# Second half of tile 0's second layer as seven quarter-size products, with its sums and those of w_out made earlier on VectorE

## The chip, the cores and the metric

The kernel runs on one core of one Trainium2 chip. A core has five engines that each run their own list of instructions in order and meet through semaphores: TensorE (PE, with its weight loads shown apart as PEld), VectorE (DVE), ScalarE (ACT), GpSimd (POOL) and SyncE (SP, which here only issues DMAs). TensorE works from SBUF into PSUM, eight banks of 2 KB for each of the 128 partitions; VectorE and ScalarE read PSUM, GpSimd does not in this kernel. The metric is the device time of one execution in microseconds; less is better.

## The reference: banded attention, then a two-layer MLP with a Gelu

Everything the kernel must compute is in these lines (q, k, v: 8 batches, 8 heads, 576 positions, 64 per head; x has 4608 tokens of 512 features; the hidden layer has 2048):

```python
scores = scale * np.matmul(q, k.transpose(0, 1, 3, 2))
mask = np.abs(pos[:, None] - pos[None, :]) <= 32
attn = softmax(np.where(mask, scores, -1e9))          # over the last axis
x = (attn @ v).transpose(0, 2, 1, 3).reshape(4608, 512)
h = x @ w_in                                          # 512 -> 2048
g = h * (1.0 / (1.0 + np.exp(-1.702 * h)))
out = g @ w_out                                       # 2048 -> 512
```

## The kernel before

**Tiles and units.** The 4608 tokens are 36 units of 128 (shifted by 32 positions, so that a unit's band of keys spans two blocks), and 9 tiles of 512, four units each. For a unit, `scores` makes q k^T on TensorE into PSUM, ScalarE takes the exponential (line 263), `band` multiplies the mask in on VectorE (line 271), `values` multiplies with v on TensorE, `norm` divides on VectorE (lines 300 and 301), and `x_T` or `x_T2` turns the result into x transposed, with a copy from PSUM.

**Layer 1** (`w_in`, Gelu). Tile 0 does it plainly (`layer1_plain`, in eight pieces d of two feature blocks each and two halves of 256 tokens). From tile 1 on, a group of features n (0 to 3) is made by `l1_group` with seven products P1 to P7 of half size in each dimension in place of eight, in the manner of Strassen and Winograd. Its operands are sums: `w1_sums` of w_in (tiles a1 to a4, in two halves), `x_sums` of x. A group uses four PSUM banks A, C, B, E. Its order on TensorE is P1 (into A), fill, P7 (into C), fill, P6 (into B), P2 (into A), fill, P5 (into B), P4 (into E), fill, P3 (into B). ScalarE copies A into B and C into an SBUF tile s7 after P7. VectorE makes e = b + s7 after P6 (line 439, called the E add) and c = b + s7 after P5 (line 445, the C add). So P5 may not write B before line 439 has read it, P3 not before line 445, and P4 needs the sum in E. ScalarE takes the four Gelus (line 426).

**Fill and side.** `fill(i)` puts matmuls of the second layer, from the list `self.l2`, behind product i; `dv` is a list of VectorE instructions, of which `fill` and `side` take the next ones at fixed places. A place in the group is also a place in VectorE's own order: what a fill adds after P1 and P7 stands ahead of the E add, what side 0 and the fill after P2 add stands between the E add and the C add.

**Layer 2** (`w_out`). For tile 0 it is plain: `layer2_plain(0, pr)` for each half pr of the token blocks, 32 matmuls of 512 columns for a half, two PSUM banks LA and LB, each copied out after its sixteenth feature block. From tile 1 on, `layer2` makes a `pair` (tile, half) by seven products of eight matmuls each, with 256 columns; it needs sums of w_out (`w2_sums`, tiles b1 to b4, two halves of 1,024 elements each) and of g (`g_sums`, which makes three sums in a tile gs and overwrites one quarter of g). A pair uses the same LA and LB, in halves: P1 and P2 add up in a, P7 in c, the others in b and e; after P7 ScalarE or VectorE (`seed2`) copies a into b and c into s7o, after P6 VectorE adds (line 519), after P2 a copy goes out (line 521), after P5 an add goes out (line 525), after P3 the 512-wide rest goes out (line 534).

**The order of the work around the change** is written out by hand (`manual_schedule`: every engine runs its instructions as the program emits them). `opening` does tile 0 up to its first layer and 24 of the 32 matmuls of its second layer's first half, with the attention of tile 1. `first_layer1` then runs the four groups of tile 1; its fills take the last eight matmuls of the first half in group 0 and 24 of the 32 of the second half in the groups 1 to 3. In VectorE's list, group 0 has the two last sums of w_in, later groups have `g_sums` of tile 1 and the eight `w2_sums`. `run` then emits the scores of units 8 and 9, the last eight matmuls of the second half, the scores of unit 10, the first twelve of the list `more` (the pairs from tile 1 on, whose first item is P1 of tile 1), the masks of units 8 and 9, and so on. GpSimd issues the loads of q, k and v (`fetch`) and makes the copies of v for odd blocks (`odd_v`, lines 216 and 217); the second layer's results leave through SP (`store`).

Of the kernel before, what the change touches and what calls it, by code (L numbers as in the profile page):

```python
# [26 lines left out]
class _Kernel:  # L27
# [333 lines left out]
        return [lambda: sub(s[:, 2], b22, b12), lambda: sub(s[:, 0], b12, b11), lambda: sub(s[:, 1], b22, s[:, 0]),  # L361
                lambda: sub(s[:, 3], b21, s[:, 1])]

    def g_sums(self, t, lo, n):

        e = self.nc.vector
        g = self.g[t]
        if t not in self.gs:
            self.gs[t] = self.sb("gs", [128, 3, 8, 256], F16, 2)
        s = self.gs[t]  # L370
        f, f2 = slice(lo, lo + n), slice(8 + lo, 8 + lo + n)
        a11, a21, a12, a22 = g[:, f, 0:256], g[:, f, 256:512], g[:, f2, 0:256], g[:, f2, 256:512]
        return [lambda: e.tensor_add(s[:, 0, f], a21, a22),
                lambda: e.tensor_sub(a21, a11, a21),
                lambda: e.tensor_sub(s[:, 1, f], s[:, 0, f], a11),
                lambda: e.tensor_sub(s[:, 2, f], a12, s[:, 1, f])]
# [122 lines left out]
    def layer2(self, pairs, last):  # L499

        dve = self.nc.vector

        def pair(t, pr, la="LA", lb="LB", end=None):
            st = {}

            def after(P):  # L510
                o = st.get("o")
                if P == 7:
                    be = self.bank(lb, name="o")
                    st.update(b=be[:, 0:256], e=be[:, 256:512], be=be, s7=self.sb("s7o", [128, 256], F32, 2),
                              o=self.sb("o_sb", [128, 2, self.DM], F32, 2))
                    self.copy(self.seed2, st["b"], st["a"])
                    self.copy(self.seed2, st["s7"], st["c"])
                elif P == 6:
                    dve.tensor_add(st["e"], st["b"], st["s7"])
                elif P == 2:  # L520
                    self.copy(self.l2eng, o[:, 0, 0:256], st["a"])
                    if end:
                        self.store_part(t, pr, o, 0, slice(0, 256), end[0])
                elif P == 5:
                    dve.tensor_add(o[:, 1, 256:512], st["b"], st["s7"])
                    if end:
                        self.store_part(t, pr, o, 1, slice(0, 512), end[0])
                elif P == 4 and end:
                    self.copy(self.nc.scalar, o[:, 1, 0:256], st["e"])
                elif P == 3 and end:  # L530
                    self.copy(end[1], o[:, 0, 256:512], st["b"])
                    self.store_part(t, pr, o, 0, slice(256, 512), end[0])
                elif P == 3:
                    self.copy(self.l2eng, o.rearrange("p i n -> p (i n)")[:, 256:768], st["be"])
                    self.store(t, pr, o)

            def part(P, f):
                if P == 1 and f == 0:
                    ac = self.bank(la, name="o")
                    st.update(a=ac[:, 0:256], c=ac[:, 256:512])  # L540
                bank = st["a" if P in (1, 2) else "c" if P == 7 else "e" if P == 4 else "b"]
                self.l2_mm(t, pr, P, f, bank, start=(P == 1))
                if f == 7:
                    after(P)

            return {P: [lambda P=P, f=f: part(P, f) for f in range(8)] for P in (1, 7, 6, 2, 4, 5, 3)}

        ps = [pair(*x) for x in pairs[:-1]] + [pair(*pairs[-1], end=(self.nc.sync, dve))]
        out = ps[0][1] + ps[0][7]
        for x, y in zip(ps, ps[1:]):  # L550
            out += x[6] + x[2] + x[4] + x[5] + y[1] + x[3] + y[7]
        x, y = ps[-1], pair(*last, "A", "B", (self.nc.scalar, self.nc.scalar))
        out += y[1] + y[7]
        for P in (6, 2, 4, 5, 3):
            out += x[P] + y[P]
        return out
# [12 lines left out]
    def opening(self):  # L569

        nc, dve, act, pool = self.nc, self.nc.vector, self.nc.scalar, self.nc.gpsimd
# [56 lines left out]
        h, n, gelus = [], [0], []  # L628

        def l1(half, *ds):  # L630
            for d in ds:
                self.layer1_plain(0, d, half, h[n[0] % len(h)])
                n[0] += 1
# [66 lines left out]
        h[:] = "BE"  # L700
        n[0] = 0
        l1(1, 6, 7)
        self.x_T2(4, "A", act)
        self.do(self.l2, 4)
        self.x_T2(6, "t", dve)
# [11 lines left out]
    @staticmethod  # L717
    def do(fs, n=99):
        for _ in range(min(n, len(fs))):
            fs.pop(0)()  # L720
# [76 lines left out]

    def run(self):
        pool, act = self.nc.gpsimd, self.nc.scalar
        self.l2 = self.layer2_plain(0, 0) + self.layer2_plain(0, 1)  # L800
        self.opening()
        self.do(self.x_sums(1))
        late = self.first_layer1()
        more = self.layer2([(i, j) for i in range(1, self.NT) for j in range(2)][:-1], (self.NT - 1, 1))
        do = self.do
        self.l2eng = dve = self.nc.vector
        self.seed2 = act
        self.scores(8, "t")
        self.scores(9, "AC")
        self.turn(14)  # L810
        self.turn(15)
        do(late, 2)
        do(self.l2)
        self.l2 = more
        self.scores(10, "BE")
        do(more, 12)
        self.band(8)
        self.band(9)
        do(late)
        do(more, 4)  # L820
        self.values(8, "t")
        self.values(9, "AC")
        self.odd_v(12, pool)
        self.odd_v(13, pool)
        self.fetch(16)
        self.fetch(17)
        self.norm(8)
        self.norm(9)
        do(more, 8)
        self.band(10)  # L830
        self.scores(11, "BE")
        do(more, 8)
        self.x_T2(8, "t", act)
        self.values(10, "AC")
        self.norm(10)
        do(more, 8)
        self.scores(12, "t")
        self.scores(13, "BE")
        self.band(11)
        self.values(11, "AC")  # L840
        self.norm(11)
        do(more, 4)
        self.scores(14, "t")
        self.x_T2(10, "C", dve)
        self.scores(15, "BE")
        do(self.x_sums(2))
        self.seed2 = dve
        late = self.back(2)
        for t in range(3, self.NT):
            self.front(t, late)  # L850
            late = self.back(t)
        self.l2eng = act
        self.do(late, 2)
        self.do(self.l2, 16)
        self.do(late)
        self.do(self.l2, 999)

    def first_layer1(self):

        dv = [lambda i=i: self.w1_sums((i,), 1) for i in (2, 4)]  # L860
        for n in range(4):
            if n == 3:
                self.turn(12)
                self.turn(13)
            self.odd_v(8 + n, self.nc.gpsimd)
            self.fetch(12 + n)

            def fill(i):
                self.do(self.l2, {1: 1, 7: 1, 2: 3, 4: 3}[i])
                self.do(dv, {1: 2, 7: 1, 2: 0, 4: 2}[i] if n else 0)  # L870
                if i == 7 and n:
                    self.T_pe([("k8", "q8", "k9"), ("q9", "k10", "q10"), ("k11", "q11", "k12")][n - 1], self.nc.scalar)

            self.l1_group(1, n, fill, lambda i: self.do(dv, 1))
            dv += self.g_sums(1, 2 * n, 2)
            if n in (0, 1):
                dv += [lambda i=i, j=j: self.w2_sums((i,), j) for i in ((3, 1), (2, 4))[n] for j in range(2)]
        return dv

@with_exitstack  # L880
# [44 lines left out]
```

## Time and profile before

| | before |
|---|---|
| median of 3 runs | 286.68 us (286.27 to 287.21) |
| the profiled execution, its own time | 286.05 us |
| its span in the trace | 284.3 us |
| what lies around the span | 1.75 us |
| TensorE clock granted | 1.00 |
| tile 1's four groups | 46.91 to 68.50 us of the span |

A row of the timeline reads: start in us, busy time in us, engine, source line, operation, output tile from input tiles, partitions x elements and type, and how many instructions the row merges; in brackets is the idle time of the engine just before and what ended it. Line 70 is the helper that issues every matmul, so there one goes by the tiles: h is the first layer, o the second, sc scores, pv values, tp a transpose. Line 67 is the helper for copies. Matmuls are pipelined, so busy times of neighbours overlap and the distance from start to start is the cost of one.

### The profile page before, as it was taken

What the parts mean: (1) busy time and instruction counts of PE and PEld (TensorE: products, weight loads), DVE (VectorE), ACT (ScalarE), POOL (GpSimd) and SP (SyncE); (2) the same over time, 40 slices, a digit from 0 to 9 for tenths busy, and PEclk for the clock granted to TensorE, in tenths of its full rate; (3) what the DMA queues carried; (4) which work ended last, traced back from release to release, by engine and by line L of the source; (5) the groups of instructions that cost most, each with busy time, mean ns of one, the idle gap of its engine ahead of it and who ended that gap; (6) DMA issues with size and microseconds to landing.
All of it is one profiled execution on the core that took longest, in us unless ns stands there. A gap on an engine that the chain in (4) does not pass through costs nothing.

```text
span 284.3 us, 9219 instructions
## 1 busy us (share of the span) xinstructions
PE 275.4 (97%) x3818; PEld 229.8 (81%) x3818; DVE 217.0 (76%) x500; ACT 193.7 (68%) x340; POOL 128.8 (45%) x195
## 2 busy tenths in 40 slices
PE   7799999999999999999999999999999999999994
PEld 7678847776777888888888888888888888888883
DVE  1758896897887978797879887888788878945631
ACT  2467785789787769667966896588758775567410
POOL 8966467897699719749075909330110000000000
PEclk9999999999999999999999999999999999999999
DMA  7999999999999999999999999994422031201033
GB/s 93 186 193 198 186 202 158 195 124 133 133 171 154 182 130 189 150 201 147 194 106 169 141 201 106 194 112 114 130 59 94 3 111 21 76 0 74 2 112 115
DMA packets 147003, 37.38 MB, mean 131 GB/s; under 512 B 133904, under 2 KB 142608, under 8 KB 146960
## 3 DMA queue, kind: packets, MB, share of 16 engines
q0 software_dynamic: 104480, 18.42, 95.0%
q1 hardware_dynamic: 42032, 17.84, 32.6%
q8 instruction: 30, 0.49, 0.7%
q10 hardware_dynamic: 448, 0.52, 0.6%
q14 instruction: 13, 0.11, 0.1%
HBM read 36.83 MB, written 9.44 MB: 163 GB/s over the span
## 4 chain that ended last, share of the span: by engine, by line
PE 87%; DVE 4%; ACT 3%; DMA 2%; issue 1%; POOL 1%; DVEq 0%; ACTq 0%; POOLq 0%
PE h L70 39%; PE o L70 37%; PE pv L70 4%; PE sc L70 3%; DMA ve<-in_v_dram 2%; DVE p L271 2%; DVE x L301 1%; ACT p L263 1%; PE tp L329 1%; ACT L263 1%; PE junk L70 1%; PE tp L189 1%; PE tp L239 1%; POOL ve L199 1%; ACT g L426 1%
## 5 line engine op out<-in xcount | busy, mean ns | idle before, releaser
L426 ACT ACTIVATE g<-h 128x512 f16<-128x512 f32 x128 | 72.2, 598 | 35.8 <-PE h L70 35.0
L70 PEld LDWEIGHTS <-g 128*128 128x128 f16 x576 | 54.3, 98 | 9.9 <-DMA w<-in_moe_w_out_dram 0.4
L70 PEld LDWEIGHTS <-a 128*128 128x128 f16 x512 | 49.3, 97 | 10.9 <-issue 0.8
L70 PE MATMUL h<-xs,a 128*128 128x256 f16 x384 | 57.6, 272 | 0.1
L70 PE MATMUL o<-w,g 128*128 128x256 f16 (+1 forms) x320 | 55.3, 294 | 0.1
L70 PEld LDWEIGHTS <-w 128*128 128x128 f16 x512 | 48.9, 98 | 6.8 <-DVE xT L67 0.2
L70 PE MATMUL h<-xT,w 128*128 128x256 f16 x384 | 54.0, 273 | 0.0
L199 POOL DMA_DIRECT2D ve<-in_v_dram x39 | 33.3, 857 | 37.8 <-issue 30.8
L70 PEld LDWEIGHTS <-gs 128*128 128x128 f16 x384 | 36.8, 98 | 5.3 <-issue 0.4
L263 ACT ACTIVATE p<-sc 128x512 bf16<-128x512 f32 x72 | 36.7, 617 | 3.2 <-PE sc L70 3.1
L70 PE MATMUL o<-b,gs 128*128 128x256 f16 x256 | 37.7, 273 | 0.5 <-ACT o L67 0.5
L70 PE MATMUL o<-b,g 128*128 128x256 f16 x256 | 37.3, 273 | 0.0
L439 DVE TENSOR_TENSOR h<-h,s 128x512 f32<-128x512 f32 x32 | 22.3, 698 | 18.5 <-PE h L70 18.5
L67 ACT COPY h<-h 128x512 f32<-128x512 f32 x32 | 18.8, 588 | 15.9 <-PE h L70 15.5
L131 POOL DMA_DIRECT2D qst<-in_q_dram x35 | 28.1, 805 | 2.3 <-DMA w<-in_moe_w_out_dram 1.7
L131 POOL DMA_DIRECT2D kst<-in_k_dram x31 | 26.5, 856 | 5.7 <-DMA ve<-in_v_dram 3.9
L301 DVE TENSOR_TENSOR x<-pv,rec 128x256 f16<-128x256 f32 (+1 forms) x53 | 27.6, 520 | 1.8
L271 DVE TENSOR_TENSOR p<-p,mask 128x1024 bf16<-128x1024 bf16 x36 | 24.6, 687 | 4.1 <-ACT p L263 4.1
L445 DVE TENSOR_TENSOR h<-h,s 128x512 f32<-128x512 f32 x32 | 22.4, 700 | 4.7 <-PE h L70 4.2
L216 POOL COPY vo<-ve 64x264 int32<-64x264 int32 x29 | 14.0, 482 | 25.8 <-PE pv L70 24.7
L67 ACT COPY s<-h 128x512 f32<-128x512 f32 x32 | 19.2, 599 | 1.3
L70 PE MATMUL h<-xs,w 128*128 128x256 f16 x128 | 19.2, 273 | 0.0
(86 smaller groups left out, 367.6 us busy)
## 6 DMA issues: line engine op xcount, KB each, us to landing
out_dram<-o_sb SPq DMA_DIRECT2D x33, 256.0 KB, 4.0
ve<-in_v_dram POOLq DMA_DIRECT2D x31, 128.0 KB, 6.5
kst<-in_k_dram POOLq DMA_DIRECT2D x25, 128.0 KB, 6.5
qst<-in_q_dram POOLq DMA_DIRECT2D x21, 128.0 KB, 5.9
w<-in_moe_w_in_dram POOLq DMA_DIRECT2D x4, 512.0 KB, 8.2
w<-in_moe_w_out_dram POOLq DMA_DIRECT2D x4, 512.0 KB, 12.3
qst<-in_q_dram POOLq DMA_DIRECT2D x7, 96.0 KB, 6.7
ve<-in_v_dram POOLq DMA_DIRECT2D x10, 64.0 KB, 7.9
```

The lines of the kernel that those rows point to most:

```text
L67: (eng.copy if eng is self.nc.scalar else eng.tensor_copy)(out, in_)
L70: self.nc.tensor.matmul(out, lhsT, rhs, start=start, stop=stop, skip_group_check=True)
L131: self.nc.gpsimd.dma_start(t[off:off + n], src[b, :, s:s + n, :].rearrange("h s d -> s h d"))
L189: self.nc.tensor.transpose(tp[64 * (h % 2):64 * (h % 2) + 64, h // 2, j, :], src[:, 4 * i + h, j, :], self.ident)
L199: self.nc.gpsimd.dma_start(t[off:off + n, :, :self.D], self.v[b, :, s:s + n, :].rearrange("h s d -> s h d"))
L216: eng.tensor_copy(words(vo[64:128]), words(self.ve[u % 9][64:128]))
L263: self.nc.scalar.activation(p[:, eo].rearrange("k h s -> k (h s)"), sc[eo], AF.Exp, scale=self.scale)
L271: (eng or self.nc.vector).tensor_mul(pv, pv, msk.to_broadcast([128, 8, 2, SQ]))
L301: dve.tensor_mul(x[:, 4 * at:4 * (at + n), :].rearrange("p (b h) d -> p b h d", b=n), acc[:, :, :, :D], r.to_broadcast([128, n, 4, D]))
L426: act.activation(g[:, f, 256 * half:256 * half + 256], bank.rearrange("p (i n) -> p i n", i=2), AF.Gelu_apprx_sigmoid)
L439: dve.tensor_add(e, b, s7)
L445: dve.tensor_add(c, b, s7)
```

## The change

Tile 0's second half (token blocks pr = 1) is made like the later tiles: `self.l2` holds `layer2_plain(0, 0)` alone, and `layer2` now also builds a pair (0, 1) whose 56 matmuls of 256 columns (`self.lead`, in the order P1, P7, P6, P2, P4, P5, P3) come after it. `g_sums` gets a column offset and width, and makes the sums of tile 0 for the half's 128 columns in two calls of four feature blocks, each with four VectorE instructions of 512 elements: one call in `opening`, after the last pieces of tile 0's first layer, one at the head of `dv`. The list `dv` starts with these four, then `w2_sums` of b3, the two sums of w_in, and the other six `w2_sums`, then `g_sums` of tile 1 as they come. Group 0 takes five of them in place of two; the later groups take one more each, in the fill after P2. A fill of the groups 1 to 3 takes twice as many matmuls, of half the columns. In the groups, VectorE's list runs: group 0, four quarter sums and a first b3; group 1, the second b3, two sums of w_in ahead of the E add, two of b1 ahead of the C add, then three of b2 and b4; group 2, the last of b4 and then `g_sums` of tile 1.

```diff
-    def g_sums(self, t, lo, n):
+    def g_sums(self, t, lo, n, p=0, w=256):
...
-        s = self.gs[t]
+        s = self.gs[t][:, :, :, p:p + w]
...
-        a11, a21, a12, a22 = g[:, f, 0:256], g[:, f, 256:512], g[:, f2, 0:256], g[:, f2, 256:512]
+        a11, a21, a12, a22 = g[:, f, p:p + w], g[:, f, 256 + p:256 + p + w], g[:, f2, p:p + w], g[:, f2, 256 + p:256 + p + w]
...
+        x = pair(0, 1)
+        self.lead = x[1] + x[7] + x[6] + x[2] + x[4] + x[5] + x[3]
...
         l1(1, 6, 7)
+        self.do(self.g_sums(0, 0, 4, 128, 128))
         self.x_T2(4, "A", act)
...
-        self.l2 = self.layer2_plain(0, 0) + self.layer2_plain(0, 1)
+        self.l2 = self.layer2_plain(0, 0)
+        more = self.layer2([(i, j) for i in range(1, self.NT) for j in range(2)][:-1], (self.NT - 1, 1))
+        self.seed2 = self.l2eng = act
         self.opening()
...
-        dv = [lambda i=i: self.w1_sums((i,), 1) for i in (2, 4)]
+        self.l2 += self.lead
+        dv = self.g_sums(0, 4, 4, 128, 128)
+        dv += [lambda j=j: self.w2_sums((3,), j) for j in range(2)]
+        dv += [lambda i=i: self.w1_sums((i,), 1) for i in (2, 4)]
+        dv += [lambda i=i, j=j: self.w2_sums((i,), j) for i in (1, 2, 4) for j in range(2)]
...
-                self.do(self.l2, {1: 1, 7: 1, 2: 3, 4: 3}[i])
-                self.do(dv, {1: 2, 7: 1, 2: 0, 4: 2}[i] if n else 0)
+                self.do(self.l2, {1: 2, 7: 2, 2: 6, 4: 6}[i] // (1 if n else 2))
+                self.do(dv, {1: 2, 7: 1, 2: 1, 4: 2}[i] if n else {1: 0, 7: 0, 2: 1, 4: 2}[i])
...
-            if n in (0, 1):
-                dv += [lambda i=i, j=j: self.w2_sums((i,), j) for i in ((3, 1), (2, 4))[n] for j in range(2)]
```

More of the change, by code (lines that the diff above doesn't have):

```diff
@@ L803, in run @@
         late = self.first_layer1()
-        more = self.layer2([(i, j) for i in range(1, self.NT) for j in range(2)][:-1], (self.NT - 1, 1))
         do = self.do
         self.l2eng = dve = self.nc.vector
-        self.seed2 = act
         self.scores(8, "t")
```

## The prediction

> **What bounds the kernel now.** I read the page first, then busy time by stretch, then PE, DVE and ACT in order of time from 43 to 78 us, where the change lies. The page gives TensorE nearly the whole span:
>
> ```profile
> PE 275.4 (97%) x3818; PEld 229.8 (81%) x3818; DVE 217.0 (76%) x500; ACT 193.7 (68%) x340; POOL 128.8 (45%) x195
> ```
>
> The next view has a row for each stretch; these two are the groups 1 and 2 of the four feature groups of tile 1's first layer, group 0 to group 3. The columns are length, then busy time and count of PE, PEld, DVE, ACT, POOL, then clock. PE fills each stretch at clock 1.00, but DVE is busy 4.60 of 5.63 us in group 1 and 5.20 of 5.60 in group 2: about 1.0 and 0.4 us are free.
>
> ```profile
> 51.74:57.37 5.63, 5.61 (x50) 4.19 (x48) 4.60 (x10) 4.90 (x10) 4.89 (x8) 1.00 1.99 206
> 57.37:62.97 5.60, 5.60 (x50) 4.19 (x48) 5.20 (x10) 4.82 (x10) 5.44 (x9) 1.00 1.40 118
> ```
>
> DVE runs its list in the written order, and two of its instructions in each group gate PE: line 439 (the "E add", reads bank B after product P6) must end before P5 writes B, and line 445 (the "C add", after P5) before P3. PE in groups 1 and 2 (start, length, operation):
>
> ```profile
> 52.36 0.38 PE L70 MATMUL o<-w,g 128*128 128x512 f16 x1
> 52.57 0.60 PE L70 MATMUL h<-xs,a 128*128 128x256 f16 x4
> 53.89 0.60 PE L70 MATMUL h<-xs,a 128*128 128x256 f16 x4
> 55.41 0.60 PE L70 MATMUL h<-xs,a 128*128 128x256 f16 x4
> 56.93 0.60 PE L70 MATMUL h<-xT,a 128*128 128x256 f16 x4
> 57.37 0.60 PE L70 MATMUL h<-xT,w 128*128 128x256 f16 x4
> 59.35 0.60 PE L70 MATMUL h<-xs,a 128*128 128x256 f16 x4
> 60.22 0.81 PE L70 MATMUL o<-w,g 128*128 128x512 f16 x3
> 61.02 0.60 PE L70 MATMUL h<-xs,a 128*128 128x256 f16 x4
> 62.54 0.60 PE L70 MATMUL h<-xT,a 128*128 128x256 f16 x4
> ```
>
> In group 1, P7 starts at 52.57, P6 at 53.89, P5 at 55.41 and P3 at 56.93: P6 to P5 and P5 to P3 are 1.52 us each when nothing waits. In group 2 they are 59.35, 61.02 and 62.54: P6 to P5 took 1.67. The DVE rows, with idle time before an instruction in brackets:
>
> ```profile
> 50.42 0.70 DVE L445 TENSOR_TENSOR h<-h,s 128x512 f32<-128x512 f32 x1 [0.16 <-PE h L70]
> 51.02 0.68 DVE L343 TENSOR_TENSOR a<-w,a 128x1024 f16<-128x1024 f16 x1
> 51.62 1.28 DVE L67 COPY o_sb<-o 128x512 f32<-128x512 f32 x2
> 54.60 0.70 DVE L439 TENSOR_TENSOR h<-h,s 128x512 f32<-128x512 f32 x1 [0.57 <-PE h L70]
> 56.05 0.70 DVE L445 TENSOR_TENSOR h<-h,s 128x512 f32<-128x512 f32 x1 [0.43 <-PE h L70]
> 56.66 2.90 DVE L353 TENSOR_TENSOR b<-w 128x1024 f16<-128x1024 f16 x4
> 59.49 0.41 DVE L373 TENSOR_TENSOR gs<-g 128x512 f16<-128x512 f16 x1
> 60.27 0.69 DVE L439 TENSOR_TENSOR h<-h,s 128x512 f32<-128x512 f32 x1
> ```
>
> The E add of group 2 at 60.27 had no idle time before it: DVE came late to it from four sums of w_out, and P5 could start only at 61.02, 0.74 after the add. The three matmuls before P5 start at 60.22 and need 0.64 (1.52 less two products of 0.44, the distance 56.93 to 57.37), so PE lost about 0.15 us. This sets the rules I use: E add no sooner than P6 + 0.71 (53.89 to 54.60), C add no sooner than P5 + 0.64 (55.41 to 56.05), and each lets P5 or P3 go 0.74 after its start. The same 0.74 separates the first copy at 51.62 from PE's 52.36, which needed the bank that it frees.
>
> **The change part by part.** *The products.* Removed are 32 matmuls of 512 columns, added 56 of 256. In the groups 1 to 3 each fill keeps its length (two of 256 for one of 512); all of the gain lies in the last piece, where eight of 256 take the place of these eight of 512:
>
> ```profile
> 67.99 0.60 PE L70 MATMUL h<-xT,a 128*128 128x256 f16 x4
> 69.15 1.90 PE L70 MATMUL o<-w,g 128*128 128x512 f16 x8
> 70.98 0.45 PE L70 MATMUL sc<-qT,kT 64*64 64x64 bf16 x24
> 71.40 1.03 PE L70 MATMUL o<-w,g 128*128 128x256 f16 x8
> 72.27 1.04 PE L70 MATMUL o<-b,g 128*128 128x256 f16 x8
> ```
>
> 69.15 to 70.98 less a small gap is 1.7 us; eight of 256 take 0.87 (71.40 to 72.27): 0.83 us of PE work goes.
>
> *Four quarter sums in the opening.* DVE waits there 2.21 us for PE:
>
> ```profile
> 46.25 0.69 DVE L67 COPY xT<-tp 128x1024 f16<-128x1024 f16 x1 [2.21 <-PE tp L329]
> ```
>
> A sum of 512 elements takes 0.39 from start to start (59.49 to 60.27 above is two, one after the other), taken as 0.40, four 1.6: hidden, cost 0. They write into the buffer that tile 0's staged q and k left, whose last readers are the scores of unit 3, long done. Uncovered they cost at most 0.4: at 0.66 each, as one such sum took at 69.26 (row below), they end at 46.67.
>
> *Group 0.* Its two sums of w_in go later. In the order of the new code, after the C add at 50.42 DVE has one quarter sum (51.02 to 51.42) in place of 0.60 of w_in. So the two copies that free banks LA and LB start at 51.42, not 51.62. LA is free at 52.16 and PE, ready at 52.18 (group 1's P1 ran its 0.44 from 51.74), no longer waits: 0.18 gained.
>
> *Group 1.* DVE's list between the C add of group 0 and the E add of group 1 is now: quarter sum, two copies, quarter sum, then w_out, w_out, w_in, w_in with 1,024 elements each. At 0.60 each (51.02 to 51.62): 51.42 + 1.20 + 0.40 + 4 x 0.60 = 55.42. P6 is due at 53.71 and its E add at 54.42, so the add is 1.0 late, and P5 goes at 55.42 + 0.74 = 56.16 in place of 55.41. PE stands still 0.9 us; queued behind P5 on PE are P4, the fill and P3, behind the add on DVE two sums of w_out and the C add. Those two sums start at 56.02. I take them at 0.71, the mean of the four at 56.66 (to 59.49), because they fall beside the same two copies on POOL, which begin at 56.69 (below, with shortest, median and longest ns of the two lines):
>
> ```profile
> 56.69 0.92 POOL L216 COPY vo<-ve 64x264 int32<-64x264 int32 x1
> L216 POOL COPY vo<-ve x29: 407/408/920, 19.6 to 210.0; 64x264 int32<-64x264 int32 x29
> L217 POOL COPY vo<-ve x28: 402/403/760, 20.1 to 199.7; 64x264 int32<-64x264 int32 x28
> ```
>
> The C add starts at 57.44, P3 at 58.18 against 56.93. Running total: 1.25 us late. At 0.60 per sum it would be 1.03.
>
> The Trainium skill (SBUF — State Buffer, Who interferes with whom) says that a VectorE instruction with two SBUF inputs and a GpSimd one that reads SBUF lock each other out for a whole instruction. By it the two POOL copies could come before the C add as a whole, which is rival 3 below, and the sum would be +1.7 in place of +1.1. The four sums at 56.66 lost 0.43 in all (2.83 against 2.40), which bears out the contention, not the full price here.
>
> *Group 2.* P1 at 58.62, P6 1.98 later (57.37 to 59.35) at 60.60, E add due at 61.31. DVE after the C add: four sums of w_out (2.4) and two of tile 1 (0.8), to 61.24: in time, so the 0.15 wait of before is gone and P5 starts at 62.12. From 61.91 DVE has a sum, the new 256-wide add (0.34, as 75.98 to 76.31 below), a sum: C add at 63.05, P3 at 63.79, against 62.54: still 1.25.
>
> *Group 3* holds five sums, the two adds and a new 256-wide add, some 3.6 us in 5.5: no stall, P3 at 69.2 against 67.99.
>
> *ACT* gets three 256-wide copies (0.45 each by the row at 73.90 below) and loses one of 512. The two seeds in group 1 stand ahead of the Gelu of bank C, but that one waits for the late C add; next P7 needs C at 59.28, it is free at 59.2. Taken at 0; without that cover, up to 0.3. *Queues*: no DMA is added; the half tile's store leaves SP after a copy at the end of P3, as it did after the last of the eight, and only a later use of its buffer waits for it: 0.
>
> *The end of the stage*, in the times of before:
>
> ```profile
> 70.54 2.07 ACT L263 ACTIVATE p<-sc 128x512 bf16<-128x512 f32 x4
> 72.46 0.62 ACT L67 COPY o_sb<-o 128x512 f32<-128x512 f32 x1
> 73.90 0.45 ACT L67 COPY o<-o 128x256 f32<-128x256 f32 x1
> 74.40 1.03 PE L70 MATMUL o<-b,gs 128*128 128x256 f16 x8 [0.46 <-ACT o L67]
> 69.26 0.66 DVE L373 TENSOR_TENSOR gs<-g 128x512 f16<-128x512 f16 x1 [0.67 <-ACT g L426]
> 72.64 0.69 DVE L271 TENSOR_TENSOR p<-p,mask 128x1024 bf16<-128x1024 bf16 x1 [0.22 <-ACT p L263]
> 75.98 0.42 DVE L519 TENSOR_TENSOR o<-o,s7o 128x256 f32<-128x256 f32 x1
> 76.31 0.68 DVE L271 TENSOR_TENSOR p<-p,mask 128x1024 bf16<-128x1024 bf16 x1
> 77.17 0.22 PE L70 MATMUL pv<-ve,p 128*64 128x65 bf16 x1
> ```
>
> PE already waits here (0.46) for ACT, whose four exps, behind a table load, PE's shorter list doesn't touch: they follow the last Gelu, which follows P3. The copy at 72.46 leaves ACT, so the seed and the P6 behind it come 0.45 sooner. But the mask at 72.64 still waits for the exps, and DVE's list from it to the mask at 76.31 is unchanged; unit 10's values, at 77.17 before, need that mask: 76.31 + 0.73 = 77.04. Of 0.83, 0.13 stays (0.45 if DVE's list runs shorter). From 80 us on PE's longest wait for another engine is this row, so nothing absorbs the shift:
>
> ```profile
> PE tp L329 <- DVE x L301: 0.2, 1, 0.2
> ```
>
> **Sum.** +1.25 (the late adds, gains of 0.18 and 0.15 inside) - 0.13 = +1.1 us. On the profiled execution, 286.05 us, that is 287.15; that execution lies 0.63 under the median of the runs, 286.68, so for the median 287.8. Its own bounds: low 1.0 - 0.45 = +0.55 (287.2); high 1.25 + 0.4 = +1.65 (288.3).
>
> **The rivals.**
> 1. *The adds stay in time*: DVE passes its longer list quickly enough that neither add reaches PE. It takes 0.9 us less than my 4.4 us ahead of the E add of group 1; for it speaks only that 0.57 and 0.43 were idle there. Then -0.18 - 0.15 - 0.13 = about -0.5: 286.2.
> 2. *Faster*: the values of unit 10 are not what holds the end of the stage, PE keeps the whole 0.83 and DVE is in time as in 1: -0.83 - 0.33 = -1.16, 285.5. It decides if the mask at 76.31 can start 0.7 sooner; the unbroken DVE list from 72.64 speaks against it.
> 3. *Slower still*: DVE stands still ahead of the C add of group 1 for both POOL copies at their shortest, 0.41 + 0.40, of which 0.71 per sum holds 0.22: +0.6, with up to 0.4 on top where the opening's sums aren't hidden: +1.7 to +2.1, 288.4 to 288.8. For it speaks POOL's slow copy of 0.92; against it, that the four sums beside it lost only 0.43. By the rule of the Trainium skill (SBUF — State Buffer, Who interferes with whom) it would come out so.
>
> **How the numbers follow.** Forecast 0.60 (its range 287.2 to 288.3), rival 1 0.15, rival 2 0.08, rival 3 0.17. A difference of 0.3% is 0.86 us, about what this kernel's measurement can tell; +0.86 is 287.54, so of the forecast's 0.60 some 0.43 is slower and 0.17 the same. Slower 0.60, same 0.32, faster 0.08. The range leaves out rival 2 and what rival 3 may hold above its sum: 286.2 to 288.8.
>
> **What would show it.** Right: in group 1 both adds with no idle time before them, starts of P6 and P5 some 2.4 us apart (1.52 unhindered), P5 and P3 some 2.0; the piece after the scores of unit 9 half as long, PE idle before the values of unit 9. The groups' four stretches together some 1.2 us longer. Wrong: if the adds of group 1 keep idle time before them, if the 1,024-element sums take another time than 0.6, or if PE's idle time between 68 and 78 us shrinks by more than 0.5.

## The result, and the profile after

| | before | after |
|---|---|---|
| median of 4 runs each, on one chip | 286.48 us (286.10 to 287.21) | 288.54 us (288.25 to 288.94) |
| the profiled execution | 286.05 us | 288.25 us |
| its span | 284.3 us | 286.5 us |

The ratio is 1.0073 (95% interval 1.0048 to 1.0097): slower by 2.1 us. In the experiments below the same two kernels ran again with more runs and gave 1.0080 (1.0055 to 1.0105). The forecast was 287.8 us, +1.1. The time lies inside the whole range (to 288.8), but above the bounds of the sum itself (287.2 to 288.3), and half of the increase is not in that sum.

The page of the kernel after: PE is as busy as before (275.1 us against 275.4), in a span that is 2.2 us longer. So the time went into waits of PE and into the end, not into matmuls.

```profile
PE 275.1 (96%) x3842; PEld 231.8 (81%) x3842; DVE 221.5 (77%) x510; ACT 194.0 (68%) x342; POOL 127.3 (44%) x195
```

First the place where the two traces start to differ. Up to group 1 they run at a fixed distance: from the last wait of PE for a mask in the opening (42.15 before, 41.80 after) to group 1's P1 it is 9.59 us before and 9.58 after. That the kernel after has this wait 0.35 earlier lies ahead of all the change touches; over the profiled executions of this study P1 of group 1 starts anywhere from 51.38 to 52.84, with the opening's waits for loads. The following comparisons go from P1. One row of the timeline of after belongs to the quarter sums in the opening:

```profile
45.89 0.69 DVE L67 COPY xT<-tp 128x1024 f16<-128x1024 f16 x1 [0.62 <-PE tp L329]
```

VectorE still waits 0.62 us for PE ahead of that copy, where it waited 2.21: the four sums ahead of the copy took 1.6 of idle time and nothing else.

**The groups.** Busy time by stretch of the kernel after, groups 1 and 2 (length, then PE, PEld, DVE, ACT, POOL, clock):

```profile
51.38:58.25 6.87, 5.79 (x58) 4.96 (x56) 6.84 (x12) 5.25 (x12) 6.41 (x11) 1.00 2.08 199
58.25:63.85 5.60, 5.60 (x60) 5.08 (x58) 5.53 (x13) 5.02 (x11) 5.50 (x8) 1.00 1.47 110
```

DVE has become the engine that fills group 1: 6.84 of 6.87 us, where it was 4.60 of 5.63. PE in the same view as before, in order of time:

```profile
52.04 0.60 PE L70 MATMUL h<-xs,a 128*128 128x256 f16 x4
53.36 0.60 PE L70 MATMUL h<-xs,a 128*128 128x256 f16 x4
55.81 0.60 PE L70 MATMUL h<-xs,a 128*128 128x256 f16 x4 [0.76 <-DVE h L439]
57.82 0.60 PE L70 MATMUL h<-xT,a 128*128 128x256 f16 x4 [0.32 <-DVE h L445]
60.23 0.60 PE L70 MATMUL h<-xs,a 128*128 128x256 f16 x4
61.76 0.60 PE L70 MATMUL h<-xs,a 128*128 128x256 f16 x4
63.29 0.60 PE L70 MATMUL h<-xT,a 128*128 128x256 f16 x4
68.79 0.60 PE L70 MATMUL h<-xT,a 128*128 128x256 f16 x4
```

P6 to P5 of group 1 is 2.45 us (53.36 to 55.81), P5 to P3 2.01. In group 2 the same two distances are 1.53 and 1.53, so nothing waits there any more. VectorE's rows show why:

```profile
50.67 0.42 DVE L375 TENSOR_TENSOR gs<-gs,g 128x512 f16<-128x512 f16 x1
51.00 1.28 DVE L67 COPY o_sb<-o 128x512 f32<-128x512 f32 x2
52.20 0.41 DVE L376 TENSOR_TENSOR gs<-g,gs 128x512 f16<-128x512 f16 x1
52.53 1.29 DVE L353 TENSOR_TENSOR b<-w 128x1024 f16<-128x1024 f16 x2
53.74 0.68 DVE L342 TENSOR_TENSOR a<-a,w 128x1024 f16<-128x1024 f16 x1
54.46 0.69 DVE L343 TENSOR_TENSOR a<-w,a 128x1024 f16<-128x1024 f16 x1
55.07 0.69 DVE L439 TENSOR_TENSOR h<-h,s 128x512 f32<-128x512 f32 x1
55.67 1.49 DVE L353 TENSOR_TENSOR b<-w 128x1024 f16<-128x1024 f16 x2
57.08 0.69 DVE L445 TENSOR_TENSOR h<-h,s 128x512 f32<-128x512 f32 x1
```

Eight instructions without a gap stand between the C add of group 0 and the E add at 55.07, which has no idle time before it; nor has the C add at 57.08. Both adds let PE go 0.74 after they start. From group 1's P1 to the last P3 it is 17.41 us (51.38 to 68.79), against 16.25: **+1.16**.

**The end of the stage.** Rows of several engines from the same timeline of the kernel after:

```profile
69.95 1.05 PE L70 MATMUL o<-w,gs 128*128 128x256 f16 x8
70.93 0.45 PE L70 MATMUL sc<-qT,kT 64*64 64x64 bf16 x24
...
74.04 0.63 DVE L375 TENSOR_TENSOR gs<-gs,g 128x512 f16<-128x512 f16 x1
74.71 0.51 DVE L376 TENSOR_TENSOR gs<-g,gs 128x512 f16<-128x512 f16 x1
...
77.40 0.68 DVE L271 TENSOR_TENSOR p<-p,mask 128x1024 bf16<-128x1024 bf16 x1
78.14 0.22 PE L70 MATMUL pv<-ve,p 128*64 128x65 bf16 x1 [0.59 <-DVE p L271]
...
83.33 1.19 DVE L361 TENSOR_TENSOR xs<-xT 128x512 f16<-128x512 f16 x2
...
85.75 0.70 DVE L439 TENSOR_TENSOR h<-h,s 128x512 f32<-128x512 f32 x1
```

The piece after the scores of unit 9 takes half as long (69.95 to 70.93 in place of 69.15 to 70.98), and PE gives it back waiting for masks: 0.46 us ahead of the values of unit 9 (74.18) and 0.59 at 78.14, for that of unit 10. Measured from group 3's P3, that mask stands at 8.61 (8.32 before: 76.31 less 67.99) and tile 2's first E add at 16.96 (85.75 less 68.79). In the timeline of the kernel before, the x_sums, that add and the last copy of all on ScalarE:

```profile
82.36 0.76 DVE L361 TENSOR_TENSOR xs<-xT 128x512 f16<-128x512 f16 x2
...
84.38 0.68 DVE L439 TENSOR_TENSOR h<-h,s 128x512 f32<-128x512 f32 x1
...
280.52 0.37 ACT L67 COPY o_sb<-o 128x256 f32<-128x256 f32 x1 [3.12 <-PE o L70]
```

There the add stands 16.39 after P3: **+0.57** where the prediction has -0.13. The x_sums alone took 1.19 in place of 0.76.

**The end of the span.** After, the last copy stands at 282.06:

```profile
282.06 0.37 ACT L67 COPY o_sb<-o 128x256 f32<-128x256 f32 x1 [3.12 <-PE o L70]
```

The span ends 3.78 later before and 4.44 later after, **+0.66**, though the work behind it is the same copy and the same 128 KB store, which ScalarE issues (ACTq). The DMA view from the issue of that store to the end, before and after (bytes moved in 40 equal slices, and the store's size and its us to landing):

```profile
GB/s 292 292 255 304 328 268 231 110 37 0 194 340 340 365 243 73 0 0 97 0 0 0 0 0 0 0 0 0 0 0 0 0 0 0 0 0 97 0 0 0
...
out_dram<-o_sb ACTq DMA_DIRECT2D x1, 128.0 KB, 1.7
```

```profile
GB/s 304 244 284 304 254 304 71 20 71 314 345 324 193 41 20 20 0 10 30 10 0 0 0 0 0 0 0 0 0 0 0 0 0 0 0 0 0 81 0 0
...
out_dram<-o_sb ACTq DMA_DIRECT2D x1, 128.0 KB, 2.4
```

A slice is 0.084 us before and 0.101 after. The bulk of the store is through in about as long; after, a rest of at most some 40 GB/s drags on for seven slices, some 0.7 us. It is not this store alone: the 128 KB store that SP issues 0.8 us sooner lands 2.0 us after its issue before and 2.7 after.

The balance of the two spans: -0.36 (P1 of group 1, within what the opening varies by) + 1.16 (groups) + 0.57 (end of the stage) + 0.17 (from there to the last copy) + 0.66 (end) = +2.2. The second pair of profiles (the two kernels again, below) gives -0.36, +1.16, +0.59, 0.00 and +0.61, together +2.0 (285.4 to 287.4 us).

### The profile page after: what moved, and what is told of

It reads as the page before. It is cut to its first block, busy times and chain, and to the rows that moved or that the text cites. A ratio compares the mean times of both kernels' runs of the same rounds, so it can differ in the third digit from the quotient of the medians.

```text
span 286.5 us, 9279 instructions
## 1 busy us (share of the span) xinstructions
PE 275.1 (96%) x3842; PEld 231.8 (81%) x3842; DVE 221.5 (77%) x510; ACT 194.0 (68%) x342; POOL 127.3 (44%) x195
## 4 chain that ended last, share of the span: by engine, by line
PE 78%; DVE 8%; DMA 5%; POOL 4%; ACT 2%; issue 2%; DVEq 0%; ACTq 0%; POOLq 0%
PE o L70 35%; PE h L70 35%; PE pv L70 3%; DMA w<-in_moe_w_in_dram 3%; PE sc L70 2%; POOL ve L199 2%; DMA kT<-kst 1%; DVE kq L67 1%; DVE p L271 1%; DVE x L301 1%; DVE b L353 1%; ACT L263 1%; POOL kq L143 1%; PE tp L329 1%; ACT p L263 1%
## 5 line engine op out<-in xcount | busy, mean ns | idle before, releaser
L70 PE MATMUL o<-w,g 128*128 128x256 f16 (+1 forms) x304 | 48.9, 285 | 0.0
L70 PEld LDWEIGHTS <-gs 128*128 128x128 f16 x408 | 39.0, 98 | 5.1
L70 PE MATMUL o<-b,gs 128*128 128x256 f16 x272 | 40.2, 273 | 0.1
L70 PE MATMUL o<-b,g 128*128 128x256 f16 x272 | 39.9, 273 | 0.0
L216 POOL COPY vo<-ve 64x264 int32<-64x264 int32 x29 | 13.1, 452 | 26.7 <-PE pv L70 25.3
L70 PE MATMUL o<-w,gs 128*128 128x256 f16 x136 | 19.9, 273 | 0.0
```

The lines of the kernel that those rows point to most:

```text
L70: self.nc.tensor.matmul(out, lhsT, rhs, start=start, stop=stop, skip_group_check=True)
L216: eng.tensor_copy(words(vo[64:128]), words(self.ve[u % 9][64:128]))
```

## The experiments

The theory after the result had three parts: **G**, VectorE's list in group 1 is late for two adds (+1.16); **T**, GpSimd's copies of v run beside VectorE's sums at the end of the stage (+0.6); **E**, the last store lands later (+0.6), by something other than the order of the work. The rival to G was that the extra sums cost in themselves wherever they stand; to T, that PE's shorter list shifts the stage's order; to E, that the late stage as a whole does it. In the table, "groups" is P1 of group 1 to P3 of group 3, "rest" from there to tile 2's first E add, "end" from the start of the last copy to the end of the span, all from the profiles; ratios are to the kernel before on the same chip (median 286.31 or 286.32; 286.83 for the last two rows). The runs of the kernel before reach further up than down (285.7 to 289.4), so a ratio can differ from that of the medians by up to 0.2%.

| kernel | median us | ratio (95%) | groups | rest | end |
|---|---|---|---|---|---|
| before / before again | 286.05 / 287.15 (one each) | | 16.25 / 16.26 | 16.39 / 16.39 | 3.78 / 3.8 |
| after again | 288.66 | 1.0080 (1.0055 to 1.0105) | 17.42 | 16.98 | 4.41 |
| before, two more sums | 286.78 | 0.9999 (0.9978 to 1.0020) | 16.58 | 16.39 | 3.82 |
| after, list dealt evenly | 287.53 | 1.0044 (1.0020 to 1.0067) | 16.29 | 16.98 | 4.5 |
| after, four copies of v left out | 288.10 | 1.0060 (1.0034 to 1.0086) | 17.41 | 16.35 | 4.46 |
| before, four matmuls left out | 286.40 | 1.0001 (0.9980 to 1.0022) | 16.50 | 16.47 | 3.81 |
| before, padded | 287.69 | 1.0035 (1.0015 to 1.0055) | 16.46 | 16.39 | 4.41 |
| after, evenly dealt, early seed, copies later | 287.54 | 1.0038 (1.0020 to 1.0055) | 17.58 | 16.24 | 3.99 |
| before, padded on PE / DVE / ACT | 286.67 / 286.75 / 287.47 (one each) | | 16.26 / 16.25 / 16.26 | 16.38 / 16.40 / 16.40 | 3.83 / 3.84 / 4.4 |
| after, evenly dealt, copies later | 286.70 | 0.9996 (0.9981 to 1.0011) | 16.29 | 16.24 | 4.43 |

**The two kernels again**, unchanged, for the spread between executions.

> The kernel before, unchanged, once more, for a second trace of it. If the 0.36 us by which the changed kernel reached group 1 sooner (51.38 against 51.74) and the 0.66 us that its span lost after the last matmul (PE ended 1.54 later, the span 2.2 later) only vary from execution to execution, this trace differs from the first one of before by as much at these two places, and agrees with it within 0.1 us between group 1 and the end of PE. If they belong to the change, both agree with the first trace of before within 0.1.

> The changed kernel, unchanged, in five rounds. Theory of the late adds plus POOL contention: 2.0 us over before (0.7%), and in its trace again 1.1 to 1.2 us lost in the groups 1 to 3 and some 0.7 between group 3 and the second tile's groups, where sums on DVE fall beside POOL's copies of v. If the contention is chance of one execution, the second part is between -0.1 and 0.2 and the total about 1.2 over before.

Groups and rest repeat to within 0.02 us and the end to within 0.03, so the +0.6 at the end belongs to the kernel and not to one execution; the start of group 1 and the whole span move, by 1.1 and 0.9 to 1.1 us. What the two pairs don't agree on is the 0.17 between tile 2's first E add and the last copy. So the stage lengths are the sharper measure, and the times are their check.

**Dealing VectorE's list evenly.** The same sums, but as many ahead of each add as there is time for: in group 1 the two sums of w_in and one of w_out go behind the C add, in group 2 one more of w_out goes behind each of the two adds, and tile 1's sums follow later. Two smaller edits go with it: P2 of the lead pair stands ahead of P6, and all but two of tile 1's sums that are left over stand ahead of the scores of unit 10. Neither touches what group 1 does up to its C add:

```diff
-        self.lead = x[1] + x[7] + x[6] + x[2] + x[4] + x[5] + x[3]
+        self.lead = x[1] + x[7] + x[2] + x[6] + x[4] + x[5] + x[3]
...
-        do(late, 2)
+        do(late, len(late) - 2)
...
-        dv += [lambda j=j: self.w2_sums((3,), j) for j in range(2)]
-        dv += [lambda i=i: self.w1_sums((i,), 1) for i in (2, 4)]
-        dv += [lambda i=i, j=j: self.w2_sums((i,), j) for i in (1, 2, 4) for j in range(2)]
+        dv += [lambda i=i, j=j: (self.w2_sums if i < 5 else self.w1_sums)((i % 5,), j)
+               for i, j in ((3, 0), (3, 1), (1, 0), (1, 1), (2, 0), (7, 1), (2, 1), (9, 1), (4, 0), (4, 1))]
...
-                self.do(dv, {1: 2, 7: 1, 2: 1, 4: 2}[i] if n else {1: 0, 7: 0, 2: 1, 4: 2}[i])
+                self.do(dv, ({1: 0, 7: 0, 2: 1, 4: 2}, {1: 1, 7: 0, 2: 0, 4: 2}, {1: 1, 7: 1, 2: 0, 4: 2}, {1: 2, 7: 2, 2: 1, 4: 2})[n][i])
```

> The changed kernel with DVE's list dealt out evenly: in group 1 one w_out sum ahead of the E add (the two w_in sums go behind it), one ahead of the C add, the rest and tile 1's sums later; P2 of the quarter products ahead of P6, so that its sums have longer. The same work on every engine. Theory of the late adds: the E add of group 1 waits for PE again (0.2 to 0.4 us idle before it), P6 to P5 is 1.5 us, the groups 1 to 3 take 16.2 to 16.4 us in place of 17.4, and the time is 1.0 to 1.2 under the changed kernel's, within 0.5 us of before on either side. Rival, that the products or ACT's seeds cost the time: no gain, the groups still take 17 us or more.

The adds of groups 1 and 2 wait for PE again, and P6 to P5 and P5 to P3 of group 1 are 1.53 us each; VectorE's rows of group 1 in this kernel:

```profile
54.48 0.70 DVE L439 TENSOR_TENSOR h<-h,s 128x512 f32<-128x512 f32 x1 [0.18 <-PE h L70]
...
55.94 0.70 DVE L445 TENSOR_TENSOR h<-h,s 128x512 f32<-128x512 f32 x1 [0.17 <-PE h L70]
```

The groups take 16.29, so 1.13 of the 1.16 is gone with the same sums in the same kernel: G stands, and the rival (sums cost wherever they are) falls. The time falls by 1.1 us (288.66 to 287.53), as much. It stays 1.2 over the kernel before, where 0.5 at most was expected: the rest (16.98) and the end (4.5) are still the long ones. One thing came up in place of the stall. PE and ScalarE in group 2's first products of this kernel:

```profile
57.73 0.38 PE L70 MATMUL o<-w,g 128*128 128x256 f16 x2
58.23 0.60 PE L70 MATMUL h<-xs,a 128*128 128x256 f16 x4
```

```profile
57.03 0.36 ACT L67 COPY o<-o 128x256 f32<-128x256 f32 x1
57.30 0.38 ACT L67 COPY s7o<-o 128x256 f32<-128x256 f32 x1
57.56 1.10 ACT L426 ACTIVATE g<-h 128x512 f16<-128x512 f32 x2
```

P7 starts 0.50 after the fill where two matmuls need 0.22. The two seeds (the copies at 57.03 and 57.30) stand on ScalarE ahead of the Gelu that frees bank C: this is the "up to 0.3" that the prediction kept for the case that the late C add no longer covers them.

**Two more sums in the kernel before**, put ahead of the E add of group 1 (two of b3 a second time):

```diff
+                if n == 1 and i == 7:
+                    for j in range(2):
+                        self.w2_sums((3,), j)
```

> The kernel before with two more w_out sums of 1,024 elements (a repeat of b3) on DVE ahead of the E add of group 1; nothing else. They take 1.2 us where DVE had 0.57 idle. Theory of the late adds: the E add starts at 55.2 in place of 54.6, P5 at 56.0 in place of 55.4, and 0.55 us goes through to the end: 0.5 to 0.6 us over before. Rival, that DVE has enough room behind (0.43 idle before the C add, more in group 3): nothing, within 0.1 us of before.

PE of this kernel:

```profile
56.78 0.60 PE L70 MATMUL h<-xs,a 128*128 128x256 f16 x4 [0.32 <-DVE h L439]
```

P6 to P5 grew from 1.52 to 2.00, with the wait at the same add. But the groups grew by 0.33, not 0.48 or the expected 0.55: VectorE's four sums of w_out behind the C add slid past the first of GpSimd's two copies, took 2.69 in place of 2.90, and group 2's wait of 0.15 went. A stall of this size is under what the times can tell (0.9999, interval of 0.4%), so only the trace speaks here.

**The copies of v of units 13 and 14 left out**, in the kernel after:

```diff
-            if u + n + 2 < self.NU:
+            if 14 < u + n + 2 < self.NU:
...
-        self.odd_v(13, pool)
```

> The changed kernel without POOL's copies of v for the odd blocks of units 13 and 14 (these units' odd blocks then use old values; the rest is computed as before). Theory of the contention: the last two sums of tile 1's group 3 take 0.42 each again (0.63 and 0.51 with the copies), the first two x sums of tile 2 0.76 together (1.19 with them), and from group 1's start to tile 2's first E add it is 33.7 us in place of 34.4; the time is 0.6 to 0.7 under the changed kernel's. Rival, that these rows are slow for a reason of their own: the sums stay as slow, and the time stays within 0.2.

VectorE's late sums and x_sums of this kernel:

```profile
74.25 0.42 DVE L375 TENSOR_TENSOR gs<-gs,g 128x512 f16<-128x512 f16 x1
74.71 0.43 DVE L376 TENSOR_TENSOR gs<-g,gs 128x512 f16<-128x512 f16 x1
...
83.25 0.76 DVE L361 TENSOR_TENSOR xs<-xT 128x512 f16<-128x512 f16 x2
```

Without the copies the sums take 0.42 and 0.43 in place of 0.63 and 0.51, the pair at 83.25 0.76 in place of 1.19, and the rest 16.35 in place of 16.96. T stands. The time fell by 0.56 (288.66 to 288.10, a little under the 0.6 to 0.7 expected), though the two intervals overlap.

**Four of the last eight matmuls left out of the kernel before**, 0.85 us of PE work at the place where the change saves 0.83:

```diff
+            if not (pr and f in (12, 13)):
                 self.mm(st[i], self.g[t][:, f, lo:lo + 128], self.w2[:, f, :], start=(f == 0))
```

> The kernel before with four of the eight 512-column matmuls left out that stand between the scores of units 9 and 10 (feature blocks 12 and 13 of tile 0's second half are not added). PE has 0.85 us less to do there, and nothing else changes. Theory, that this place is held by ScalarE's exps and by DVE's list up to the mask of unit 10: the mask stays at 8.3 us after P3 of group 3, PE's idle time before the values of units 8 and 9 and the next P6 grows by about 0.8, and no more than 0.15 us is gained up to tile 2's first E add (32.5 to 32.65 from group 1's start). Rival, that PE's list holds the place: 31.8 to 31.9, and 0.8 us under before.

PE of this kernel, with the two waits at this place:

```profile
71.66 0.38 PE L70 MATMUL o<-w,g 128*128 128x256 f16 x2 [0.46 <-DVE o_sb L67]
...
75.04 1.03 PE L70 MATMUL o<-b,gs 128*128 128x256 f16 x8 [0.57 <-ACT o L67]
```

The first wait is new, the second was 0.46 before, and the P6 that it stands ahead of starts 6.41 us after P3 in both kernels (75.04 less 68.63, 74.40 less 67.99): by there all of the 0.85 is gone. The rest is 16.47 against 16.39 (the groups' 16.50 is ahead of the edit, a wait for the first copy as in the next kernel): PE work at this place is worth nothing. That is the part of the prediction's last term that held. The values of unit 8 came 0.39 sooner here, GpSimd's copies of unit 13 0.38 sooner, and one sum beside them took 0.51 in place of 0.42: a small form of what part T is about, from a shorter list of PE alone.

**The kernel before, padded** with as many instructions as the change adds: 24 tiny matmuls, 10 tiny memsets on VectorE, two tiny exponentials on ScalarE, all in the opening where PE waits anyway.

```diff
-        act.activation(self.spark, self.spark, AF.Exp)
+        for _ in range(3):
+            act.activation(self.spark, self.spark, AF.Exp)
...
+        self.keep_busy(24, "E", 16)
+        for _ in range(10):
+            dve.memset(self.v_first[:, :, self.D:], 1.0)
```

> The kernel before with as many more instructions on PE (24 matmuls of 16 columns), DVE (10 tiny memsets) and ScalarE (2 tiny exps) as the change adds, all in the opening, where PE waits for the first load. In three traces of the changed kernel and its even version the last store took 2.3 to 2.4 us from issue to landing and 4.4 to 4.5 us passed from the last copy to the end of the span; in three of the kernel before and its variant 1.7 and 3.8. If the number of instructions (how the program lies) decides this, the padded kernel shows 2.3 or more and 4.4; if something in the changed kernel's work does, it shows 1.7 and 3.8. The rest, from group 1's start to the last copy, stays at 228.8 in both cases.

The end is 4.41 with before's work in before's order, and the last store takes 2.4 us to land: the end is not the late stage's doing. The time rose by 1.0 us or more, more than the 0.6 at the end. Another 0.2 is in the groups, where a sum of w_in ahead of the first copy took 0.89 (at 51.34; 0.68 before, at 51.02) and PE waited for that copy. The rest of it is not placed.

**The padding split by engine**, each part alone.

> The kernel before with the 24 tiny matmuls of the padded kernel alone, put in the opening where TensorE waits. Asked: which engine's number of instructions made the last store land 2.3 to 2.4 us after the last copy in the padded kernel and in the kernel after, and 1.7 in the kernel before. If it is TensorE's, this kernel's span ends 4.4 us after its last copy; if not, 3.8. The stretch from the first P1 to tile 2's first E add stays at 32.6 to 32.9.

> The kernel before with ten tiny memsets on VectorE alone. If VectorE's number of instructions sets how late the last store lands, the span ends 4.4 us after the last copy here and 3.8 in the two others.

> The kernel before with two tiny exponentials on ScalarE alone. ScalarE issues the last store. If ScalarE's number of instructions sets how late it lands, the span ends 4.4 us after the last copy here and 3.8 in the two others. If it ends at 3.8 in all three, no engine's count does it alone.

One trace of each, and only the one with two more instructions on ScalarE has the long end. The DMA view of that kernel from the issue of the last store on:

```profile
GB/s 338 236 266 359 307 246 92 21 61 297 338 369 205 41 31 0 10 20 20 0 0 0 0 0 0 0 0 0 0 0 0 0 0 0 0 0 82 0 0 0
```

It has the slow rest of the kernel after, and its last store lands in 2.3; those of the other two land in 1.7, and their spans end 3.83 and 3.84 after the last copy. The single times (287.47 against 286.67 and 286.75) tell nothing: those of the kernel before on this chip go from 285.98 to 287.96. The kernel after has two more instructions on ScalarE too (342 against 340, from the pages). Over the 14 traces of this study, the six with 340 end at 3.78 to 3.84, and of the eight with 342 seven end at 4.40 to 4.50. It isn't the number alone: the eighth, the kernel of the next run, ends at 3.99. SP's store ahead of the last one lands late with it (2.6 to 2.8 in those seven, 1.9 to 2.0 in the six, 2.2 in the eighth). What it is about ScalarE's list that holds up the rest of both stores stays open.

**Evenly dealt, with two further edits**: the copy of a (the seed) right after P1 of the lead pair, so that it is out of the Gelu's way, and GpSimd's copies of v for the units 13 and 14 put later in its list.

```diff
-                if P == 7:
+                if P == (1 if early else 7):
...
                     self.copy(self.seed2, st["b"], st["a"])
+                if P == 7:
                     self.copy(self.seed2, st["s7"], st["c"])
...
-        x = pair(0, 1)
...
+        x = pair(0, 1, early=True)
...
+            if t == 2 and n == 0:
+                self.load_kq("q", 18)
+                self.odd_v(14, self.nc.gpsimd)
+                self.load_kq("k", 19)
+                self.load_v(19)
...
+        self.fetch(16)
         self.odd_v(13, pool)
-        self.fetch(16)
         self.fetch(17)
```

> The even version with two more edits: the seed of the quarter products' b is copied right after P1, so that ScalarE has one copy less ahead of the Gelu of bank C in group 1 (in the even version P7 of group 2 started 0.3 late for it), and POOL's copies of v for units 13 and 14 are issued one fetch later and one load later, beside DVE's divisions, which read PSUM. Theory: the late sums and x sums run at 0.4 each, group 2 loses nothing, and from group 1's start to tile 2's first E add it is 32.2 to 32.6 us (before 32.6, even version 33.3); with 0.6 lost at the end of the span as in all versions of the changed kernel, the time lies 0.2 to 0.6 over before. If the end is lost only by chance, it is 0 to 0.4 under before.

PE in group 1 of this kernel:

```profile
57.28 0.38 PE L70 MATMUL o<-b,g 128*128 128x256 f16 x2 [1.12 <-ACT o L67]
```

The early seed failed. P7 of the lead pair writes the other half of the bank that the copy reads, and was held until the copy (56.81 to 57.23), which ScalarE reaches behind three copies of transposes and a Gelu: 1.12 us of PE, as much as the stall that the even dealing had removed. Groups and rest come to 33.82 where 32.2 to 32.6 was expected, and the time is 1.1 or 1.2 us over the kernel before (by the ratio or the medians) in place of 0.2 to 0.6. The later copies of v did what they should (rest 16.24). Whether the chip or the program's own order of the tile asks for this wait, this run doesn't tell.

**Evenly dealt, copies of v later, without the early seed.**

> The evenly dealt kernel, and GpSimd's copies of v for units 13 and 14 issued later, behind the sums that they run beside. If the kernel after lost its time to the groups (1.1 us) and to sums on VectorE beside GpSimd's copies (0.6 us), both are gone: the groups take 16.3 and the rest of the stage to tile 2's first E add 16.25, together 32.5 against 32.6 before, and the time is the end of the span's 0.6 above the kernel before: 286.9, or 0.6 under the evenly dealt kernel. If the end of the span comes to 3.8 here, 286.3. If the sums are not slowed by those copies, the time stays at the evenly dealt kernel's 287.5.

Groups 16.29 and rest 16.24, together 32.53 against 32.64 before: both losses are gone (the pair of x_sums takes 0.76 again), and with them the whole difference in time, 0.9996 (0.9981 to 1.0011). With the copies of units 13 and 14 out of the way the rest is 0.15 under that of before, about the 0.13 that the prediction's last term forecast. By the trace it should stand 0.5 above the kernel before, for the end is still 4.43; by the medians it is 0.1 below, with an interval that ends at +0.3; by the lowest time of each, 286.30 and 285.98, it is 0.3 above. So parts G and T are confirmed in time; part E is not, for the interval leaves out the 0.5 that the trace asks for, and the new order is no faster than the kernel before: 0.83 us of PE work saved, and nothing gained that can be measured.

## Why the prediction was right, and where not

**The group 1 term, right.** Counted from P1 of group 1, the E add was put at 3.68 (55.42 less 51.74) and came at 3.69; P5 at 4.42 and 4.43; the C add at 5.70 and 5.70; P3 at 6.44 and 6.44. The even dealing shows that it is this order, and not the sums themselves, that costs. That the E add came within 0.01 is in part luck: each of the two quarter sums took 0.33 from start to start where 0.40 was put, one sum of w_in (53.74 to 54.46) 0.72 where 0.60 was, and the two errors cancel.

**The sums beside GpSimd's copies, right in size.** The two sums of w_out at 55.67 took 1.49, 0.20 over the 1.29 of the pair at 52.53, which ran alone; 0.22 had been taken. Rival 3 put the whole of both copies there, which did not happen. The Trainium skill (SBUF — State Buffer, Who interferes with whom) has the two engines lock each other out for a whole instruction; the traces agree on the contention, but not on its size: 0.20 was lost at 55.67 beside two copies of 0.46 and 0.75, and 0.43 at 83.33 beside two of 0.41 and 0.48.

**The opening, group 0, group 2, group 3: right.** The opening's sums were hidden. P1 to P7 of group 1 shrank from 0.83 to 0.66 (0.18 expected). Group 2's wait went, and its P3 came 11.91 after P1 of group 1, where 12.05 was put. P3 of group 3 came at 17.41 after P1, against 17.46 (69.2 less 51.74).

**The end of the stage, wrong**: -0.13 was forecast, +0.57 measured. That PE's 0.83 would be absorbed held, and leaving out as much work in the kernel before gained nothing. What failed is the sentence that VectorE's list "from it to the mask at 76.31 is unchanged": its instructions are, their durations are not. GpSimd's copies of unit 13 wait for the values of unit 8 on PE. As PE's list got shorter, these came 0.77 sooner, counted from P3 (73.24 less 67.99 before, 73.27 less 68.79 after), and with them the copies, onto the two sums at 74.04 and 74.71, which before started at 73.25 and 73.70, with the copies at 73.82. PE, VectorE and GpSimd before:

```profile
73.24 0.22 PE L70 MATMUL pv<-ve,p 128*64 128x65 bf16 x1
73.25 0.42 DVE L375 TENSOR_TENSOR gs<-gs,g 128x512 f16<-128x512 f16 x1
73.70 0.42 DVE L376 TENSOR_TENSOR gs<-g,gs 128x512 f16<-128x512 f16 x1
73.82 0.57 POOL L216 COPY vo<-ve 64x264 int32<-64x264 int32 x1 [4.18 <-PE pv L70]
```

PE and GpSimd after, where the copy starts ahead of both sums:

```profile
73.27 0.22 PE L70 MATMUL pv<-ve,p 128*64 128x65 bf16 x1
73.86 0.54 POOL L216 COPY vo<-ve 64x264 int32<-64x264 int32 x1 [4.73 <-PE pv L70]
...
83.30 0.41 POOL L216 COPY vo<-ve 64x264 int32<-64x264 int32 x1
83.76 0.48 POOL L217 COPY vo<-ve 64x264 int32<-64x264 int32 x1
```

The next copies, of unit 14 (83.30 and 83.76), met the x_sums in the same way. The saving itself moved the contention: it cost 0.17 up to the values of unit 10 and 0.40 in the x_sums. With the copies issued later (and VectorE's list dealt evenly) the term is -0.15, about as forecast. Rival 3 named the mechanism and sought it in group 1 alone.

**ScalarE's seeds, right with its condition.** They cost 0 under the late C add (P7 of group 2 follows its fill by 0.22, 58.69 to 58.91), and 0.3 in the evenly dealt kernel, where that cover was gone.

**The end of the span, not seen.** The working ends where PE takes the shift to the end unabsorbed, and takes what follows as constant. +0.61 to +0.66 lies there, in stores whose work is the same; no run here shows why.

**Rivals 1 and 2** fall: both adds have no idle time before them, and the mask of unit 10 came no sooner.

**In sum**, groups +1.16 (forecast +1.25), end of the stage +0.57 (-0.13), end of the span +0.6 (0). The first is the mechanism forecast; the other two are as large together. That the time landed inside the range is luck: +2.1 lies above the sum's own bounds (+0.55 to +1.65), where only rival 3 (+1.7 to +2.1) had stretched the range, and what rival 3 put there, both copies ahead of the C add of group 1, did not happen.

## What to carry to other kernels

Where an engine's list is in a fixed order, count its work up to each instruction that another engine waits for, not over the stage: here VectorE had 1.0 us free in the group and was still 1.0 us late at one add. When work is taken off the bounding engine, follow every engine that waits for it as a clock (GpSimd's copies here) and ask what it will now run beside. Compare the two traces stage by stage from an anchor ahead of the change, for start and end of a span can move by half a microsecond for reasons that have nothing to do with the stage.

## What the runs showed of the hardware that was not expected

- Two tiny instructions more on ScalarE, in the opening, went with a last store that lands 2.3 us after its issue in place of 1.7, SP's store ahead of it 2.6 in place of 2.0, and a span that ends 4.4 in place of 3.8 after the last copy; 24 more matmuls or 10 more VectorE instructions did not (3.83, 3.84). These are one trace each; six other traces with the same count on ScalarE ended at 4.41 to 4.50 and one at 3.99. The cause is open.
- A VectorE sum of 512 elements with both inputs in SBUF took 0.63 and 0.51 beside GpSimd's copies and 0.42 and 0.43 without them; a copy of GpSimd took 0.75 beside two sums of w_out against 0.40 alone. The VectorE adds of the first layer, which read PSUM, kept their 0.68 to 0.70 in all of these kernels.
